# Block products for the upper halves from slice 6 on, and a 64-bit conversion that works in place

## The chip, the cores and the metric

One core of a Trainium2 chip runs the kernel in one launch. The time is the device time of an execution in microseconds. Before the change it is 1780.66 us, the median of three runs (1780.54 to 1782.24).

## The reference

An attention whose softmax runs over the feature axis for q and over the sequence for k makes 2304 tokens of 512 features. A mixture of 8 experts follows, all of them applied to all tokens, weighted by a matrix that eight alternating normalizations make. Last comes a gated feed-forward. All inputs are drawn as below and then cast; `w_in` and `w_out` are 64-bit floats, since they are divided by a 64-bit root.

```python
kv = np.einsum('bhsd,bhse->bhde', k_s, v)
x = np.einsum('bhsd,bhde->bhse', q_s, kv)            # 2304 x 512
for e in range(8):                                   # w1[e] 512 x 1024, w2[e] 1024 x 512
    out += P[:, e:e + 1] * (np.maximum(x @ w1[e], 0.0) @ w2[e])
h = out @ w_in                                       # 512 x 2048, then w_out 2048 x 512
y = (h * np.clip(h + 3.0, 0.0, 6.0) / 6.0) @ w_out
```

## The kernel before

Both feed-forward parts are cut into 20 slices of 512 hidden columns: 16 of the experts (`NE`), 4 of the last layer. For each slice the 18 groups of 128 tokens are taken as three pairs of two groups of 384 tokens. Here a *step* is one pair in one slice; step 14.1 is the second pair taken in slice 14, counted from 0. All operands are float32 numbers split into two float16 halves, an upper and a lower one, so a product is upper x upper plus the two cross products.

The product with W1 (`ups`, L1689) always uses seven block products of half size in place of eight (Strassen-Winograd), in two bursts of seven units a step, 6 matmuls of 384 columns a unit. Each burst leaves four results in float32 rooms (`ring_r`, or parts of `scr`): ACT reads two banks and DVE adds the others. They are split into halves in *ring h*, 16 rooms of two halves, 384 columns each: an upper half by ACT, a lower one by POOL or DVE.

The product with W2 (`downs_fast`, L1867) belongs to the step before and stands between the units of the present one. It uses the seven block products for the cross terms in all of `FAST`. The upper x upper terms are multiplied directly (`main`, L1899), except in the slices of `FULL`, 11 to 14 (L508). There the sums of blocks are made in float32 and split (`whole`, L1766; for W2 `t_sums`, L1458, from sums that POOL leaves in `raw`), and `cross` takes three matmuls a term where it else takes two, without `main`:

```python
def main(o, grp, cols):
    if whole_sums(s, p):
        return
    for fc in range(4):
        nc.tensor.matmul(
            o, hs[grp][fc][:, 0, ts_], w[:, 0, fc, cols], start=False, stop=(fc == 3), skip_group_check=True
        )
```

Whole sums need more rooms, and take six of them in `scr` (L1759). In a FULL slice `raw` holds the float32 sums of W2 up to the end of the slice's first step, so the next weights are prepared one step later in the slice (`when`, L2197).

The 64-bit weights of the last layer are turned to 32 bits on the way, in 32 pieces of 128 x 512 (`conv_steps`, L827): a load into `scr`, four DVE operations, two of ACT, one multiplication on POOL and a store to DRAM (`win`, `wout`). All pieces use the same room. They hang in the queue `back`, from which `tick` (L614) takes one entry on two beats of three; a step has 28 beats. They must be over before slice 16 loads its weights from the result.

Nothing is issued at once: a planner (`Planner`, L73) records every operation with the matmul clock at which it was recorded, finds what depends on what, and lists them by due time with a cost for each form. Background operations (`filling`) are put in only where the due ones behind them still fit (L372), or when their own due time is near. All instructions therefore carry line 471, and the engines run them in the planned order.

Of the kernel before, what the change touches and what calls it, by code (L numbers as in the profile page):

```python
# [474 lines left out]
def tile_attention_moe_ffn(  # L475
# [17 lines left out]
    P = 128  # L493
# [13 lines left out]
    ALSO = ((15, 0), (16, 2))  # L507
    FULL = range(11, 15)  # L508
    PAIRS = [(0, 1), (3, 4), (2, 5)]
# [46 lines left out]
    def psm(shape, name, dt=F32):  # L556
        return bank_of("m", shape)

    def rt(name):
        return ring("r", [P, GN], F32, 6)  # L560
# [245 lines left out]
    def w2_steps(s, flat=raw):  # L806
        st = {}
        dst = w2op[s % 2]
        rw = view(flat, 0, [P, NKC, FS])

        def load():
            nc.sync.dma_start(out=rw, in_=w2_src(s))

        def sp(c):
            return lambda: split(dst[:, 0, c], dst[:, 1, c], rw[:, c], st["s"][:, 0:1])

        steps = [load] + fill(s) + w_scale(f"b{s}_", st, w2buf[s % 2], flat)
        steps[-1] = (lambda f=steps[-1]: (f(), res[s].__setitem__("s2", st["s"])))
        steps += [sp(c) for c in range(NFC)]
        if s in FULL:  # L820
            b11, b12, b21, b22 = w2_parts
            steps += [lambda a=a: nc.gpsimd.tensor_sub(*a) for a in ((b11, b12, b11), (b12, b22, b12), (b22, b11, b22))]
            steps += [lambda: nc.gpsimd.tensor_add(b21, b21, b22)]
        return steps


    def conv_steps(src, dst, name):  # L827

        n = 512
        bits = view(scr, 0, [P, 2 * n], I32).rearrange("p (n t) -> p n t", t=2)  # L830
        hi = bits[:, :, 1]
        mid = view(scr, 0, [P, 2 * n], I32).bitcast(U16).rearrange("p (n t) -> p n t", t=4)[:, :, 1]
        m, t, g = (scr[:, (2 + i) * n : (3 + i) * n] for i in range(3))
        mi, ti = m.bitcast(I32), t.bitcast(I32)

        def load():
            nc.sync.dma_start(out=view(scr, 0, [P, n], U64), in_=src)

        def f0():
# [3 lines left out]
        def f1():  # L843
            nc.scalar.activation(ti, ti, AF.Relu, scale=8.0, bias=less)
            nc.vector.tensor_scalar(
                out=mi, in0=hi, scalar1=0xFFFFF, scalar2=0x100000, op0=ALU.bitwise_and, op1=ALU.bitwise_or
            )

        def f2():
# [4 lines left out]
        def f3():  # L854
            nc.vector.scalar_tensor_tensor(out=m, in0=mi, scalar=2.0 ** -20, in1=g, op0=ALU.mult, op1=ALU.add)

        def f4():
            nc.gpsimd.tensor_mul(m, m, t)

        def store():  # L860
            nc.sync.dma_start(out=dst, in_=m)

        return [load, None, None, f0, f1, f2, f3, f4, None, store]

    def all_conv():
        for i in range(NF):
            fs = slice(i * FS, (i + 1) * FS)
            for c in range(NKC):
                rs = slice(c * P, (c + 1) * P)
                put(back, map(filling, conv_steps(w_in[rs, fs], win32[rs, fs], f"i{i}{c}")))  # L870
            for c in range(NFC):
                rs = slice(i * FS + c * P, i * FS + (c + 1) * P)
                put(back, map(filling, conv_steps(w_out[rs, :], wout32[rs, :], f"o{i}{c}")))
        put(back, [], "conv")
# [38 lines left out]
    def attention(pr):  # L913
# [192 lines left out]
        def qtr(c, g, src=None):  # L1106
# [5 lines left out]
            if "rooms" in t:  # L1112
                qT = t["rooms"][2 + t["m"] % (len(t["rooms"]) - 2)]
            else:
                h = ring("h", [P, 2, GN], F16, HB)
                qT = h.rearrange("p a n -> p (a n)").bitcast(F32)
# [370 lines left out]
    def up_burst(s, p, qf, hs, between):  # L1487
# [36 lines left out]
        def emit(c, grp, fc, clean=False, pool=False):  # L1524
            h = ring("h", [P, 2, GN], F16, HB)
            hs[grp][fc] = h
# [162 lines left out]
    def ups(s, p, hs):  # L1689
# [23 lines left out]
        def gate_(c, grp, fc, scale, bias, top):  # L1713
            h = ring("h", [P, 2, GN], F16, HB)
# [5 lines left out]
        def gated(hg, r, c, pool=True):  # L1720
            h, g, top = hg
            nc.vector.scalar_tensor_tensor(out=r, in0=g, scalar=top, in1=c, op0=ALU.min, op1=ALU.mult)
            nc.scalar.copy(h[:, 0, :], r)
            (nc.gpsimd if pool else nc.vector).tensor_sub(h[:, 1, :], r, h[:, 0, :])

        def straight(b, grp, fc, n, t):

            hg = gate_(b, grp, fc, zd, low3, 6.0 * KAPPA * H_DOWN)
            gated(hg, t(n), b)

# [3 lines left out]
        def hi(c, grp, fc, relu):  # L1734
            h = ring("h", [P, 2, GN], F16, HB)
            hs[grp][fc] = h
# [17 lines left out]
        def burst(qf):  # L1754
            r = [rt(f"r{n}_{s}_{p}_{qf}") for n in range(0)]
            t = {}
# [9 lines left out]
            def whole(which):  # L1766

                for k in which:
# [5 lines left out]
                    elif k == 4:  # L1774
                        r = t[2]
                        if ffn:
                            nc.vector.tensor_add(r, r, t[3])
                        else:
                            nc.vector.scalar_tensor_tensor(
                                out=r, in0=r, scalar=0.0, in1=t[3], op0=ALU.max, op1=ALU.add  # L1780
                            )
                    else:
# [49 lines left out]
            def u5():  # L1832
# [10 lines left out]
            def u6():  # L1843
# [23 lines left out]
    def downs_fast(prev):  # L1867
# [497 lines left out]
```

## Time and profile before

| | before |
|---|---|
| median of 3 runs | 1780.66 us |
| profiled execution | 1781.37 us |
| its span, first to last instruction | 1779.6 us |
| TensorE busy | 1759.3 us (99%) |
| VectorE (DVE) busy | 1377.2 us (77%) |
| ScalarE (ACT) busy | 1193.9 us (67%) |
| GpSimd (POOL) busy | 543.4 us (31%) |

PE is the matmul part of TensorE, PEld its weight loads, SP the engine that issues DMAs. Busy time is the union of an engine's instructions: where two overlap it counts once. An average over the span says little, because the slices differ; so the windows below are cut where the first W1 product of a slice or step starts, and the rest of the reading is by window. A row of windows has the window's bounds and length, then busy time and instructions of PE, PEld, DVE, ACT and POOL, then the granted clock, the DMA share and GB/s. A row of a chain has start, length and what it was; a row of a group has busy time and the mean of one in ns, then the idle time ahead and what ended it.

### The profile page before, as it was taken

How to read it: one execution, taken by the hardware profiler on the slowest of the kernel's cores; microseconds unless marked ns; L12 is line 12 of the kernel's file. 1: busy time of each engine (PE TensorE's matmuls, PEld its weight loads, DVE VectorE, ACT ScalarE, POOL GpSimd, SP SyncE). 2: the span in 40 equal slices, each digit the busy share in tenths (PEclk: the TensorE clock that was granted, in tenths of full speed). 3: DMA queues.
4: the chain of work that ended last, by engine and by line, in shares of the span. 5: the costliest groups of instructions: out<-in, count | busy, mean ns of one | idle time of the engine just before them, and what ended most of it. 6: DMA issues, size and time to landing. Idle time of an engine off the chain costs nothing.

```text
span 1779.6 us, 33317 instructions
## 1 busy us (share of the span) xinstructions
PE 1759.3 (99%) x13097; PEld 1208.3 (68%) x13097; DVE 1377.2 (77%) x2550; ACT 1193.9 (67%) x2654; POOL 543.4 (31%) x513
## 2 busy tenths in 40 slices
PE   7999999999999999999999999999999999999999
PEld 5555556777777777777777777777777555777775
DVE  7874776787777778777866688888888898888774
ACT  5856475666766666766756576867787568876553
POOL 3423344324323232333222222222322223231221
PEclk9999999999999999999999999999999999999999
DMA  9410231324141423142312121120212454302031
GB/s 296 115 68 1 87 99 48 108 80 138 61 134 66 134 66 122 60 140 78 116 62 78 28 84 51 60 81 30 87 48 87 87 95 139 149 25 86 1 98 72
DMA packets 103325, 154.20 MB, mean 87 GB/s; under 512 B 47744, under 2 KB 51840, under 8 KB 102912
## 3 DMA queue, kind: packets, MB, share of 16 engines
q1 hardware_dynamic: 103168, 152.08, 27.7%
q8 instruction: 102, 1.67, 0.4%
q14 instruction: 55, 0.45, 0.1%
HBM read 119.69 MB, written 24.12 MB: 81 GB/s over the span
## 4 chain that ended last, share of the span: by engine, by line
PE 96%; DVE 2%; DMA 1%; ACT 0%; issue 0%; SPq 0%; POOL 0%; ACTq 0%; POOLq 0%
PE b L471 96%; DMA acc<-in_v_dram 0%; DMA raw<-in_moe_w_dram 0%; DVE xbuf L471 0%; DMA xbuf<-in_k_dram 0%; DMA acc<-in_q_dram 0%; DVE ring_r L471 0%; PE b L2331 0%; DVE prob L471 0%; DVE ring_c L471 0%; DVE ring_h L471 0%; DVE ring_qm L471 0%; DVE scr L471 0%; SPq L471 0%; DVE acc L471 0%
## 5 line engine op out<-in xcount | busy, mean ns | idle before, releaser
L471 PE MATMUL b<-xbuf,w1buf 128*128 128x384 f16 x5040 | 908.2, 326 | 1.9 <-ACT ring_r L471 1.2
L471 PEld LDWEIGHTS <-w1buf 128*128 128x128 f16 x5040 | 492.0, 98 | 280.2 <-issue 2.5
L471 PE MATMUL b<-w2buf,ring_h 128*128 128x256 f16 (+1 forms) x3456 | 608.5, 310 | 0.1
L471 POOL TENSOR_TENSOR ring_h<-ring_r,ring_h 128x384 f16<-128x384 f32 x312 | 299.5, 962 | 876.5 <-ACT ring_h L471 727.3
L471 PEld LDWEIGHTS <-ring_h 128*128 128x128 f16 x4116 | 401.2, 98 | 171.6 <-issue 2.1
L471 ACT COPY b<-b 128x256 f32<-128x256 f32 (+1 forms) x686 | 251.6, 375 | 257.3 <-PE b L471 162.1
L471 DVE SCALAR_TENSOR_TENSOR acc<-b,ring_cf,acc 128x512 f32<-128x512 f32 x372 | 274.8, 748 | 143.1 <-PE b L471 126.8
L471 PEld LDWEIGHTS <-xbuf 128*128 128x128 f16 x2820 | 262.9, 98 | 77.3
L471 ACT ACTIVATE ring_r<-b 128x384 f32<-128x384 f32 x384 | 187.5, 489 | 141.7 <-PE b L471 135.4
L471 DVE SCALAR_TENSOR_TENSOR ring_r<-b,ring_r 128x384 f32<-128x384 f32 x250 | 138.0, 553 | 76.4 <-ACT ring_r L471 42.1
L471 ACT ACTIVATE ring_h<-ring_r 128x384 f16<-128x384 f32 x288 | 147.9, 522 | 12.1 <-DVE ring_r L471 8.4
L471 PE MATMUL b<-xbuf 128*128 128x256 f16 (+1 forms) x1236 | 107.3, 249 | 4.1 <-issue 1.7
L471 PE MATMUL b<-kvs,xbuf 128*128 128x256 f16 x660 | 96.1, 273 | 0.0
L471 PE MATMUL b<-scr,xbuf 128*128 128x256 f16 x660 | 96.1, 273 | 0.0
L471 PE MATMUL b<-w2buf,xbuf 128*128 128x256 f16 x660 | 96.1, 273 | 0.0
L471 DVE TENSOR_TENSOR xbuf<-ring_h 128x768 f16<-128x768 f16 x148 | 91.4, 620 | 0.0
L471 DVE SCALAR_TENSOR_TENSOR acc<-b,ring_co,acc 128x512 f32<-128x512 f32 (+1 forms) x82 | 60.5, 742 | 30.7 <-PE b L471 27.6
L471 ACT CAST ring_h<-ring_r 128x384 f16<-128x384 f32 x144 | 72.0, 508 | 17.4 <-DVE ring_r L471 16.5
L471 PE MATMUL b<-xbuf,ring_h 128*128 128x256 f16 x366 | 80.0, 273 | 0.0
L471 DVE SCALAR_TENSOR_TENSOR w1buf<-raw,ring_ws,w1buf 128x512 f16<-128x512 f32 x100 | 76.3, 794 | 2.1 <-ACT w1buf L471 1.5
L471 PE MATMUL b<-lg,ring_h 128*128 128x256 f16 x294 | 74.1, 273 | 0.0
L471 ACT ACTIVATE w1buf<-raw,ring_ws 128x512 f16<-128x512 f32 x100 | 67.9, 715 | 6.6 <-DVE ring_ws L471 5.8
(185 smaller groups left out, 1802.9 us busy)
## 6 DMA issues: line engine op xcount, KB each, us to landing
xbuf<-xkeep SPq DMA_DIRECT2D x119, 384.0 KB, 3.7
raw<-in_moe_w_dram SPq DMA_DIRECT2D x31, 1024.0 KB, 5.8
scr<-in_moe_w_in_dram SPq DMA_DIRECT2D x16, 512.0 KB, 3.6
scr<-in_moe_w_out_dram SPq DMA_DIRECT2D x16, 512.0 KB, 3.4
xkeep<-xbuf SPq DMA_DIRECT2D x2, 2688.0 KB, 8.9
xkeep<-xbuf SPq DMA_DIRECT2D x14, 384.0 KB, 7.7
out_dram<-acc SPq DMA_DIRECT2D x18, 256.0 KB, 2.0
win<-scr SPq DMA_DIRECT2D x16, 256.0 KB, 2.1
```

The lines of the kernel that those rows point to most:

```text
L471: f(*a, **k)
```

## The change

`FULL` becomes slices 6 to 14. Three things follow from code that depends on it: whole sums and no `main` in slices 6 to 10, later preparation of weights for slices 6 to 11, and no room in `scr` for the conversion from slice 6 on.

- *Halves that nothing multiplies are not made.* With whole sums, block 21 of the hidden values enters sums alone, so its halves are dropped; block 12 is clipped in place by ACT, its upper half made by ACT and the lower by POOL (before: ACT, then DVE). Of W2, one quarter, block 12, enters sums alone, and the split of its rows covers half the width.
- *The conversion in place.* A piece takes 3 x 512 words where it took 5 x 512: the masks and sums go back into the strided words of the loaded numbers. Until slice 6 a piece stands in `scr`. From the third step of slice 6 it stands in the last four rooms of ring h, which `ht` keeps from the halves while `lending` is 2 or 3; with 6 halves a step instead of 8, twelve rooms hold two steps. `lend` moves the state on before each step, at slice 15 all pieces still open are recorded, and the rooms go back to ring h. While pieces are lent rooms, one entry is taken on one beat of four.

```diff
-    FULL = range(11, 15)
+    FULL = range(6, 15)
+    def ht(s):
+        if "h" not in rings:
+            rings["h"] = [cpool.tile([P, HB, 2, GN], F16, name="ring_h"), list(range(HB))]
+        r, last = rings["h"]
+        n = next(n for n in last if n < HB - 4 or lending[0] in (0, 1, 4))
+        last.append(last.pop(last.index(n)))
+        return r[:, n]
...
-        if back and beat[0] % 3:
+        if back and (chunk[0] or lending[0] in (0, 3)) and (
+            beat[0] % 4 < 1 if lending[0] else beat[0] % 3 < 2
+        ):
             pop(back)
...
+        if s in FULL and s < NS - 1:
+            left = slice(0, DM // 2)
+            steps += [sp(0), sp(1)]
+            steps += [lambda: split(dst[:, 0, 2:, left], dst[:, 1, 2:, left], rw[:, 2:, left], st["s"][:, 0:1])]
...
+                    st["at"] = scr if not lending[0] else rings["h"][0][:, HB - 4 :].rearrange(
+                        "p b a n -> p (b a n)"
+                    ).bitcast(F32)
...
-            nc.vector.scalar_tensor_tensor(out=m, in0=mi, scalar=2.0 ** -20, in1=g, op0=ALU.mult, op1=ALU.add)
+            nc.vector.scalar_tensor_tensor(out=g, in0=hi, scalar=2.0 ** -20, in1=g, op0=ALU.mult, op1=ALU.add)
...
-            nc.gpsimd.tensor_mul(m, m, t)
+            nc.gpsimd.tensor_mul(t, g, t)
...
-                    after_units(1, lambda: lo(hi(t[4], 0, qf + 2, False), t[4], False))
+                    if not full:
+                        after_units(1, lambda: lo(hi(t[4], 0, qf + 2, False), t[4], False))
...
-                    if full:
-                        lo(hi(t[2], 1, qf, True), t[2], True)
-                        return
                     nc.scalar.activation(t[2], t[2], AF.Relu)
                     lo(hi(t[2], 1, qf, False), t[2], False)
...
+    def lend(s, p):
+        n = turns[s].index(p)
+        at = 0 if s < FULL[0] else 4 if s >= 15 else min(n + 1, 3) if s == FULL[0] else 3
+        while back and at != lending[0] and (at == 4 or chunk[0]):
+            pop(back)
+        lending[0] = at
```

On PE, in slice 8, the product for the lower token group of one tile stood before as two cross matmuls a term and then the wide ones (`lg` and `xbuf` hold the two parts of T4, `w2buf` is W2, bank b_67 the sum):

```order
L471 MATMUL b_67<-lg,ring_h 128x256
L471 LDWEIGHTS ring_h
L471 MATMUL b_67<-xbuf,ring_h 128x256
L471 LDWEIGHTS ring_h
L471 MATMUL b_67<-w2buf_83,ring_h 128x512
L471 LDWEIGHTS ring_h
L471 MATMUL b_67<-w2buf_83,ring_h 128x512
```

The same place now:

```order
L472 MATMUL b_67<-lg,ring_h 128x256
L472 LDWEIGHTS ring_h
L472 MATMUL b_67<-xbuf,ring_h 128x256
L472 LDWEIGHTS ring_h
L472 MATMUL b_67<-xbuf,ring_h 128x256
L472 LDWEIGHTS ring_h
L472 MATMUL b_67<-lg,ring_h 128x256
```

The four wide matmuls are gone, and each of the two terms has a third narrow one.

On DVE, at the start of slice 15 (`acc` is the result of the W2 products, `xbuf` the halves of sums, `ring_r` and `scr` results of the W1 products, `ring_h` of 384 columns a lower half), before:

```order
L471 SCALAR_TENSOR_TENSOR acc<-b_67,ring_cf,acc 128x512
L471 SCALAR_TENSOR_TENSOR acc<-b_66,ring_cf,acc 128x512
L471 TENSOR_TENSOR ring_wsc<-ring_ws 128x1
L471 TENSOR_SCALAR ring_cf<-prob,ring_wsc 128x18
L471 TENSOR_TENSOR xbuf<-ring_r,xbuf 128x384
L471 TENSOR_TENSOR xbuf<-scr,xbuf 128x384
L471 TENSOR_TENSOR xbuf<-ring_r,xbuf 128x384
L471 SCALAR_TENSOR_TENSOR ring_h<-ring_r,ring_h 128x384
L471 SCALAR_TENSOR_TENSOR ring_h<-scr,ring_h 128x384
L471 SCALAR_TENSOR_TENSOR ring_r<-ring_r 128x384
```

Now, where `ring_h` of 512 columns is a piece of the conversion in its lent rooms:

```order
L472 SCALAR_TENSOR_TENSOR acc<-b_67,ring_cf,acc 128x512
L472 SCALAR_TENSOR_TENSOR acc<-b_66,ring_cf,acc 128x512
L472 TENSOR_SCALAR ring_ws<-ring_c1i 128x1
L472 TENSOR_TENSOR ring_wsc<-ring_ws 128x1
L472 TENSOR_SCALAR ring_cf<-prob,ring_wsc 128x18
L472 SCALAR_TENSOR_TENSOR ring_h<-ring_h 128x512
L472 TENSOR_TENSOR xbuf<-scr,xbuf 128x384
L472 TENSOR_TENSOR xbuf<-ring_r,xbuf 128x384
L472 TENSOR_SCALAR ring_h<-ring_h 128x512
L472 SCALAR_TENSOR_TENSOR ring_h<-ring_h 128x512
L472 TENSOR_TENSOR xbuf<-scr,xbuf 128x384
L472 TENSOR_TENSOR xbuf<-ring_r,xbuf 128x384
```

Three of the four operations of a piece have come in between the sums, and the two lower halves stand elsewhere or are gone.

## Rows read from the trace of the kernel before

**Rows 1.** Page, shares of the span and granted clock by slice of it

```profile
PE 1759.3 (99%) x13097; PEld 1208.3 (68%) x13097; DVE 1377.2 (77%) x2550; ACT 1193.9 (67%) x2654; POOL 543.4 (31%) x513
...
PEclk9999999999999999999999999999999999999999
```

**Rows 2.** Page, chain that ended last; then the largest group of matmuls

```profile
PE 96%; DVE 2%; DMA 1%; ACT 0%; issue 0%; SPq 0%; POOL 0%; ACTq 0%; POOLq 0%
...
L471 PE MATMUL b<-xbuf,w1buf 128*128 128x384 f16 x5040 | 908.2, 326 | 1.9 <-ACT ring_r L471 1.2
```

**Rows 3.** Windows: slices 4, 12, 13, 16, and 2 to 9 together

```profile
412.88:497.08 84.20, 84.20 (x617) 59.97 (x615) 64.76 (x118) 57.09 (x131) 27.56 (x27) 1.00 0.32 102
1083.99:1166.56 82.57, 82.49 (x634) 61.73 (x632) 69.92 (x127) 61.68 (x147) 22.83 (x20) 1.00 0.20 60
1166.56:1248.89 82.33, 82.33 (x634) 61.74 (x632) 69.66 (x128) 61.41 (x147) 23.14 (x20) 1.00 0.20 60
...
1418.67:1507.68 89.01, 88.32 (x476) 46.22 (x474) 81.75 (x161) 63.47 (x115) 26.89 (x24) 1.00 0.53 120
...
242.71:918.07 675.36, 675.36 (x4869) 475.51 (x4868) 514.14 (x924) 455.90 (x1044) 233.13 (x226) 1.00 0.30 97
```

**Rows 4.** Start of slice 15: PE's wait; first and last of the chain's DVE pieces

```profile
1342.69 1.14 PE L471 MATMUL b<-xbuf,w1buf 128*128 128x384 f16 x6 [1.19 <-ACT ring_r L471]
...
1331.42 0.19 DVE ring_r L471
...
1339.99 2.13 DVE xbuf L471 x3
```

**Rows 5.** Groups of PE by form in slice 4 (busy us, mean ns)

```profile
L471 PE MATMUL b<-w2buf,ring_h 128*128 128x512 f16 x36 | 9.2, 379 | 0.0
```

**Rows 6.** A group of DVE by form in slices 11 to 14: lower halves

```profile
L471 DVE SCALAR_TENSOR_TENSOR ring_h<-ring_r,ring_h 128x384 f16<-128x384 f32 x23 | 12.7, 568 | 0.0
```

**Rows 7.** Chain of waits in slice 12 (start, us, what)

```profile
1138.22 6.57 DMA raw<-in_moe_w_dram
```

**Rows 8.** Groups by form: conversion on DVE and POOL, dearest 512-column DVE row

```profile
L471 DVE TENSOR_SCALAR scr<-scr 128x512 int32<-128x512 int32 x60 | 29.3, 498 | 0.0
L471 DVE SCALAR_TENSOR_TENSOR scr<-scr 128x512 int32<-128x512 int32 x30 | 22.3, 745 | 4.5 <-ACT scr L471 4.5
L471 DVE SCALAR_TENSOR_TENSOR scr<-scr 128x512 f32<-128x512 int32 x31 | 21.3, 688 | 0.7
...
L471 POOL TENSOR_TENSOR scr<-scr 128x512 f32<-128x512 f32 x32 | 42.0, 1312 | 46.5 <-DVE scr L471 42.5 <-ACT ring_r L471 4.0
...
L471 DVE SCALAR_TENSOR_TENSOR scr<-raw,ring_ws,scr 128x512 f16<-128x512 f32 x4 | 3.7, 929 | 0.0
```

**Rows 9.** Windows: steps 13.2, 14.0, 14.1, 14.2, 15.0, 15.1 and 16.1

```profile
1221.44:1248.89 27.45, 27.45 (x212) 20.59 (x211) 25.03 (x49) 21.14 (x54) 4.74 (x5) 1.00 0.14 39
1248.89:1276.29 27.40, 27.40 (x212) 20.55 (x210) 22.55 (x37) 17.88 (x42) 8.75 (x8) 1.00 0.27 76
1276.29:1303.76 27.47, 27.47 (x213) 20.60 (x211) 22.08 (x43) 22.39 (x54) 9.65 (x8) 1.00 0.21 66
1303.76:1331.22 27.46, 27.46 (x213) 20.60 (x211) 24.81 (x48) 22.46 (x55) 4.14 (x5) 1.00 0.22 68
1331.22:1360.03 28.81, 27.62 (x214) 20.61 (x211) 25.92 (x47) 21.70 (x52) 10.80 (x9) 1.00 0.27 83
1360.03:1389.43 29.40, 29.40 (x219) 21.20 (x218) 22.09 (x40) 19.77 (x48) 6.61 (x8) 1.00 0.16 59
1447.92:1478.06 30.14, 29.45 (x159) 15.39 (x158) 29.04 (x64) 23.05 (x39) 7.63 (x7) 1.00 0.58 97
```

**Rows 10.** SP: first converted weights for slice 16; page: conversion DMAs

```profile
1327.38 0.37 SPq L471 DMA_DIRECT2D raw<-win  x1
...
scr<-in_moe_w_in_dram SPq DMA_DIRECT2D x16, 512.0 KB, 3.6
...
win<-scr SPq DMA_DIRECT2D x16, 256.0 KB, 2.1
```

More of the change, by code (lines that the diff above doesn't have):

```diff
@@ L59 @@
     "a1sums": -73500.0,
+    "conv": 0000.0,
     "max": 40000.0,
@@ L607, in tile_attention_moe_ffn @@
     rate = [1]
+    chunk = [False]
+    lending = [0]
     def pop(d):
@@ L818, in w2_steps @@
         steps[-1] = (lambda f=steps[-1]: (f(), res[s].__setitem__("s2", st["s"])))
-        steps += [sp(c) for c in range(NFC)]
+        if s in FULL and s < NS - 1:
+            left = slice(0, DM // 2)
+            steps += [sp(0), sp(1)]
+            steps += [lambda: split(dst[:, 0, 2:, left], dst[:, 1, 2:, left], rw[:, 2:, left], st["s"][:, 0:1])]
+        else:
+            steps += [sp(c) for c in range(NFC)]
         if s in FULL:
@@ L829, in conv_steps, with room, g, load @@
         n = 512
[L830 to L839, printed above, removed]
+        st = {}
+        def room(f):
+            def g():
+                if f is load:
+                    st["at"] = scr if not lending[0] else rings["h"][0][:, HB - 4 :].rearrange(
+                        "p b a n -> p (b a n)"
+                    ).bitcast(F32)
+                    chunk[0] = True
+                lent = st["at"]
+                bits = lent[:, : 2 * n].bitcast(I32).rearrange("p (n t) -> p n t", t=2)
+                hi = bits[:, :, 1]
+                mid = lent[:, : 2 * n].bitcast(U16).rearrange("p (n t) -> p n t", t=4)[:, :, 1]
+                g, t = bits[:, :, 0].bitcast(F32), lent[:, 2 * n : 3 * n]
+                marked(filling(lambda: f(lent, hi, mid, g, t, t.bitcast(I32))), "conv")()
+                if f is store:
+                    chunk[0] = False
+            return g
+        def load(lent, *_):
+            nc.sync.dma_start(out=lent[:, : 2 * n].bitcast(U64), in_=src)
+        def f0(lent, hi, mid, g, t, ti):
             nc.vector.tensor_scalar(out=ti, in0=hi, scalar1=0x7FF00000, scalar2=None, op0=ALU.bitwise_and)
             nc.scalar.activation(g, mid, AF.Copy, scale=2.0 ** -36)
-        def f1():
+        def f1(lent, hi, mid, g, t, ti):
             nc.scalar.activation(ti, ti, AF.Relu, scale=8.0, bias=less)
[L845 to L849, printed above, removed]
+        def f2(lent, hi, mid, g, t, ti):
             nc.vector.scalar_tensor_tensor(
@@ L852, in f2, with f3, f4, store @@
             )
-        def f3():
-            nc.vector.scalar_tensor_tensor(out=m, in0=mi, scalar=2.0 ** -20, in1=g, op0=ALU.mult, op1=ALU.add)
-        def f4():
-            nc.gpsimd.tensor_mul(m, m, t)
-        def store():
-            nc.sync.dma_start(out=dst, in_=m)
-        return [load, None, None, f0, f1, f2, f3, f4, None, store]
+            nc.vector.tensor_scalar(
+                out=hi, in0=hi, scalar1=0xFFFFF, scalar2=0x100000, op0=ALU.bitwise_and, op1=ALU.bitwise_or
+            )
+        def f3(lent, hi, mid, g, t, ti):
+            nc.vector.scalar_tensor_tensor(out=g, in0=hi, scalar=2.0 ** -20, in1=g, op0=ALU.mult, op1=ALU.add)
+        def f4(lent, hi, mid, g, t, ti):
+            nc.gpsimd.tensor_mul(t, g, t)
+        def store(lent, hi, mid, g, t, ti):
+            nc.sync.dma_start(out=dst, in_=t)
+        return [f and room(f) for f in (load, None, None, f0, f1, f2, f3, f4, None, store)]
     def all_conv():
@@ L869, in all_conv @@
                 rs = slice(c * P, (c + 1) * P)
-                put(back, map(filling, conv_steps(w_in[rs, fs], win32[rs, fs], f"i{i}{c}")))
+                put(back, conv_steps(w_in[rs, fs], win32[rs, fs], f"i{i}{c}"))
             for c in range(NFC):
                 rs = slice(i * FS + c * P, i * FS + (c + 1) * P)
-                put(back, map(filling, conv_steps(w_out[rs, :], wout32[rs, :], f"o{i}{c}")))
+                put(back, conv_steps(w_out[rs, :], wout32[rs, :], f"o{i}{c}"))
         put(back, [], "conv")
@@ L1114, in qtr @@
             else:
-                h = ring("h", [P, 2, GN], F16, HB)
+                h = ht(0)
                 qT = h.rearrange("p a n -> p (a n)").bitcast(F32)
@@ L1524, in emit @@
         def emit(c, grp, fc, clean=False, pool=False):
-            h = ring("h", [P, 2, GN], F16, HB)
+            h = ht(s)
             hs[grp][fc] = h
@@ L1713, in gate_ @@
         def gate_(c, grp, fc, scale, bias, top):
-            h = ring("h", [P, 2, GN], F16, HB)
+            h = ht(s)
             hs[grp][fc] = h
@@ L1718, in gate_, with gated @@
             return h, g, top
-        def gated(hg, r, c, pool=True):
+        def gated(hg, r, c, pool=True, split_=True):
             h, g, top = hg
             nc.vector.scalar_tensor_tensor(out=r, in0=g, scalar=top, in1=c, op0=ALU.min, op1=ALU.mult)
+            if not split_:
+                return
             nc.scalar.copy(h[:, 0, :], r)
@@ L1728, in straight @@
             hg = gate_(b, grp, fc, zd, low3, 6.0 * KAPPA * H_DOWN)
-            gated(hg, t(n), b)
+            gated(hg, t(n), b, split_=not full or n == 1)
         def around(r, grp, fc, pool=True):
@@ L1734, in hi @@
         def hi(c, grp, fc, relu):
-            h = ring("h", [P, 2, GN], F16, HB)
+            h = ht(s)
             hs[grp][fc] = h
@@ L1754, in burst @@
         def burst(qf):
-            r = [rt(f"r{n}_{s}_{p}_{qf}") for n in range(0)]
             t = {}
@@ L1775, in whole @@
                         r = t[2]
[L1776 to L1781, printed above, removed]
+                        nc.vector.tensor_add(r, r, t[3])
                     else:
@@ L1973, in downs_fast @@
         return made
+    def lend(s, p):
[4 more added lines that the diff above has]
+        lending[0] = at
     def fast_step(s, p, prev):
+        lend(s, p)
         need(("w1", s))
```

## The prediction

> **What bounds the kernel now.** I read the page's shares first, then the chain of waits, then busy time in windows cut at the first product of each 512-column slice, and last the DVE groups by form. TensorE is busy for 99% of the span and its granted clock is full from end to end, so its 2.4 GHz level holds throughout [rows 1]. The chain that ended last runs through PE for 96%, and the largest group of matmuls waited 1.9 us in the whole run [rows 2]. So PE's own columns set the time, and a helper engine matters only where it makes PE stand. The windows say how near that is. In slice 4, where the upper halves are multiplied directly, the window is 84.20 us and PE has no gap. In slice 13, as in 14, where seven block products are already used for them, it is 82.33 us, again without a gap, and DVE is busy for 85% of it (69.66 us) [rows 3]. At slice 15 PE does wait: 1.19 us for a room that ACT fills, behind ten microseconds, from 1331.4 to 1342.1 us, in which the chain has 11 pieces of DVE and no other engine [rows 4].
>
> **The columns that go.** One tile of 128 tokens in a direct slice has 7 cross products of 4 x 256 columns and the main ones of 4 x 512 and 8 x 256: 11,264 columns. With whole sums it has 7 x 6 x 256 = 10,752. The 512 columns saved are 213 ns at 2.4 GHz, and a slice has 9 tiles: 1.92 us. The 36 wide matmuls of a slice that vanish are the 512-column row of slice 4 [rows 5]. The windows give nearly the same by measurement: 84.20 - 82.33 = 1.87 us. Slices 6 to 10 change, 5 x 1.87 = 9.35 us. All of it is on PE, so all of it counts where PE doesn't wait.
>
> **What rides along in slices 6 to 12.** The work there becomes that of slices 12 to 14 without their two dead halves. In each burst the half of block 21 is not made (one ACT write, one POOL subtraction), and that of block 12 goes from one ACT and one DVE instruction to two ACT and one POOL: ACT and POOL come out even, DVE loses one row of 0.57 us per burst [rows 6], 2.3 us in four bursts. Half a W2 split per slice goes as well. DVE at 85% with no gap in slices 13 and 14 is the cover; I cost these slices at nothing. Earlier preparation of the weights moves to the second and third step of a slice, as in slices 11 to 14. There the load of one W2 slice once stood in the chain for 6.57 us and cost PE 0.08 us of slice 12 (82.49 of 82.57), because ACT had that slice's sums queued ahead of a bank copy [rows 3, 7]. Five more such slices could each show that: 0 to 2 us, and I take 0.5.
>
> **Where the conversion goes.** By the order of the changed program, 20 of the 32 pieces stay in the old room and are done in slices 2 to 5, some 6 a slice where there were some 4.4 (32 in slices 2 to 9). Slice 4 had DVE at 64.76 of 84.20 us [rows 3]; 1.6 pieces more, at 2.43 us each (below), make 68.7 us, 82%: no cost. Of the other 12, the planner puts nearly nothing into slices 6 to 12 (one instruction here and there), because a background operation only enters where the due ones behind it still fit. Then their room is due: the four rooms of ring h are wanted again in slice 15, and pieces that share one room stand one behind the other. So the order has 37 of their 48 DVE instructions in the five steps from 13.2 to 15.0 (step n.m is the m-th pair of slice n, from 0): 5, 8, 8, 8, 8. The excerpts of DVE's order shown above are one such place, and it is the very stretch of [rows 4], where DVE already sets PE's time.
>
> The sum there: one piece costs DVE two masks of 0.498, one of 0.745 and one of 0.688 us, 2.43 us, and POOL 1.31 us [rows 8]. No row shows them in the strided, in-place form. The bounds are 2.0 us (all four at the masks' 0.498) and 3.7 us (four times the dearest row of 512 elements, 0.929 us [rows 8]), which would put 9 us over full DVE into three steps, the size of rival 2. The inputs were strided before, so I take 2.43. Steps 14.1, 14.2 and 15.0 last 83.7 us and DVE is busy in them for 22.08 + 24.81 + 25.92 = 72.8 us [rows 9]. Less 2.3 us of dead halves, plus six pieces, 14.6 us, makes 85.1 us: 102% of the time there is. Steps 13.2 and 14.0: 47.6 - 2.3 + 7.9 = 53.2 of 54.9 us, 97%. The highest share a step shows is 16.1 with 29.04 of 30.14 us, 96% [rows 9], and slice 16 as a whole has 81.75 of 89.01 us, 92% [rows 3], both with 0.69 us in which PE stood. At 96.3%, 85.1 us take 88.4 us and 53.2 us take 55.2: 4.6 + 0.4 = 5.0 us over PE's time. At 91.8% they take 92.7 and 58.0 us: 9.0 + 3.1 = 12.1 us. The lower end is nothing, if DVE's lag runs out in step 15.1, which has 7 us to spare (22.09 of 29.40) and PE's rooms carry it there. Step by step the stall is one of the order in which DVE stands, so it is nearest to the row of the one crowded step, 96%; some of it can be carried over, and I take 4.5 us. ACT in 15.0 is busy for 21.70 of 28.81 us [rows 9] and gets four rows more: no bound by itself.
>
> Behind a late DVE instruction stand the additions that read a bank of PE; PE's next product into that bank is what waits. The queue of SP carries the pieces' loads and stores in front of two things: the first converted weights for slice 16, issued at 1327.38 us where their first product starts at 1418.67 [rows 10, 3], so some 85 us of cover, and the reload of the third pair in slice 15, a step of cover.
>
> **The sum.** Profiled execution: 1781.37 us (span 1779.6). -9.35 + 0.5 + 4.5 = -4.35 us, 1777.0. The median of the three runs is 0.7 us under the profiled one, so 1776.3 us.
>
> **Rivals.** (1) *The crowd costs nothing.* The planner gives each background row a place that its model thinks free, and before, all 32 pieces went through slices 2 to 9, 675.36 us in which PE had no gap [rows 3]. Against it is 102% in three steps. 1780.66 - 9.35 = 1771.3. (2) *DVE becomes the bound at 92%.* 1780.66 - 9.35 + 0.5 + 12.1 = 1783.9. For it: 1.19 us at 15.0 with DVE at only 90%. Against: only 9 pieces are crowded, and in 16.1 DVE reached 96%. (3) *The rooms come back late*, slower than before: slice 15 writes its first halves into just the four lent rooms, and ACT stands at that write, with the bank copies behind it, until POOL's last product is over and, for two of the rooms, its store has landed. The pieces go at two a step, so one that misses its turn is 27.5 / 2 = 13.7 us late; 1780.66 - 9.35 + 13.7 = 1785.0. It decides from the point where ACT reaches the first of these writes before the twelfth piece's product has ended. Against: a piece needs about 3.6 us of load, 2.4 of DVE, 1.3 of POOL and 2.1 of store [rows 8, 10], some 9.4 of its 13.7 us. (4) *Matmuls count, not columns.* The change puts 6 matmuls for every 4, 90 more in all. At 84.20 us / 617 rows = 136 ns each that would be 12.3 us more: 1793. The rows speak against it: slice 13 has 634 rows in 82.33 us, slice 4 has 617 in 84.20.
>
> The Trainium skill, in "TensorE: Matmul & The Clock Gate", section "Back-to-back issue gap", gives for streams of weight load and matmul a sustained spacing of about 81 ns at 128 columns and 131 ns at 512. An estimate for 256 columns between these is 98 ns, so six of them for four wide ones would cost 588 for 524 ns, 2.9 us more over 45 tiles, some 1783.6 us in all. The trace disagrees, by the windows just named; the other figure of that section of the Trainium skill, columns / 2.4 plus 2.5 ns, would give the 1.87 us that the windows show.
>
> **How the numbers follow.** A difference under 0.2%, 3.6 us, counts as none (what a measurement of this kernel can tell): faster is below 1777.1, slower above 1784.2. The forecast, 1774 to 1779, has 0.50; rival 1 (1770.5 to 1774) 0.25; rival 2 (1779 to 1784) 0.13; rival 3 0.10; rival 4 0.02. Two thirds of the forecast's chance lies below 1777.1: 0.33 + 0.25 = 0.58 faster. The rest of it and rival 2: 0.30 the same. Slower: 0.12. The range goes from the full saving with a little more from the lighter steps, 1770.5, to most of rival 2, 1783.
>
> **What would show it.** Windows of slices 7 to 12 should last 82.3 to 82.7 us without gaps, with DVE at 82 to 85%; if they last 84, rival 4 holds. Steps 13.2 to 15.0 should together be 3 to 6 us longer than 138.6 us, with PE's waits released by DVE or by ACT behind DVE, and DVE at 95% or more. If those steps are as long as before, the crowd was free and the forecast is too high. If one wait of over 5 us stands in 15.0 with ACT waiting to write ring h, rival 3 holds. If slices 3 to 5 get longer, the denser conversion was not free, which I have at nothing.

## The result, and the profile after

| | before | after |
|---|---|---|
| median | 1780.6 us (6 runs) | 1793.41 us (6 runs, 1792.55 to 1798.79) |
| ratio | | 1.007, 95% interval 1.0057 to 1.0083 |
| profiled execution, its span | 1781.37, 1779.6 us | 1792.56, 1790.8 us |

The change made the kernel slower by 0.7%, where 0.2% faster was forecast, and the time lies above the range of 1770.5 to 1783 us. The page of the changed kernel, against [rows 1, 2]:

```profile
PE 1756.8 (98%) x13187; PEld 1216.8 (68%) x13187; DVE 1429.6 (80%) x2632; ACT 1233.4 (69%) x2755; POOL 556.4 (31%) x503
...
PE 93%; DVE 3%; DMA 1%; ACT 1%; issue 0%; POOL 0%; SPq 0%; POOLq 0%
...
L472 PE MATMUL b<-xbuf,w1buf 128*128 128x384 f16 x5040 | 912.5, 327 | 5.2 <-DVE ring_r L472 2.6
```

PE is busy for 2.5 us less, and yet the span is 11.2 us longer: PE stands, that is, it waits for another engine. DVE is busy for 52 us more. The windows of slices 5, 8, 12, and 13 to 16, with columns as in [rows 3]:

```profile
497.00:582.13 85.13, 84.46 (x615) 59.92 (x614) 71.16 (x124) 57.76 (x135) 35.12 (x33) 1.00 0.38 116
...
747.21:829.54 82.33, 82.33 (x635) 61.72 (x633) 69.73 (x123) 60.58 (x144) 23.82 (x20) 1.00 0.20 60
1077.55:1159.88 82.33, 82.33 (x635) 61.72 (x633) 67.01 (x123) 62.80 (x147) 22.67 (x20) 1.00 0.21 60
1159.88:1243.51 83.63, 83.63 (x645) 62.88 (x644) 70.01 (x126) 62.21 (x146) 23.24 (x20) 1.00 0.23 70
1243.51:1330.26 86.75, 80.93 (x611) 59.03 (x609) 75.98 (x140) 65.61 (x152) 31.86 (x26) 1.00 0.39 115
1330.26:1426.77 96.51, 91.14 (x600) 59.02 (x598) 81.72 (x145) 61.39 (x133) 26.53 (x24) 0.96 0.41 104
1426.77:1518.88 92.11, 88.99 (x475) 46.09 (x474) 81.92 (x163) 63.57 (x115) 25.42 (x24) 1.00 0.50 115
```

Slice 8 has exactly the 82.33 us of the whole-sum slices. Slices 6 to 12 together went from 585.3 to 577.8 us (-7.5). Slices 3 to 5 went from 252.6 to 254.1 (+1.5). Slices 13 to 16 went from 341.1 to 359.0: +17.9 us, all of the loss and more; 14.2 of it are in steps 13.2 to 15.0, which took 152.8 us for the same 1056 matmuls where they took 138.6. The steps 14.1, 14.2 and 15.0, against [rows 9]:

```profile
1269.61:1300.32 30.71, 27.93 (x212) 20.57 (x211) 26.53 (x52) 23.28 (x55) 10.78 (x9) 1.00 0.36 110
1300.32:1330.26 29.94, 26.89 (x202) 19.11 (x200) 28.00 (x52) 23.98 (x56) 9.22 (x9) 1.00 0.36 102
1330.26:1368.81 38.55, 33.65 (x237) 23.73 (x235) 33.20 (x58) 27.16 (x63) 15.66 (x13) 0.91 0.41 127
```

DVE is busy for 26.53 + 28.00 + 33.20 = 87.7 us of 99.2: 88%, not 96%. By step it is 86, 94 and 86%. Inside 15.0, in windows of a few us:

```profile
1330.00:1340.00 10.00, 9.90 (x77) 7.27 (x76) 9.93 (x19) 8.75 (x22) 3.44 (x3) 1.00 0.46 155
1340.00:1345.00 5.00, 1.96 (x16) 1.03 (x13) 4.96 (x8) 2.12 (x8) 3.53 (x3) 1.00 0.13 24
1345.00:1350.00 5.00, 3.23 (x12) 1.64 (x13) 4.75 (x11) 1.76 (x4) 1.09 (x1) 0.57 0.39 134
1350.00:1352.00 2.00, 2.00 (x11) 1.36 (x10) 0.59 (x1) 1.87 (x4) 0.00 (x0) 0.50 0.00 0
```

DVE is full for 20 us (19.64 busy) while PE gets 5.2 of the ten from 1340, and right behind that DVE has next to nothing to do (0.59 of 2 us): its next additions need banks that PE could not fill. In the table of DVE's waits for 15.0 (us, times, longest) that is the largest entry:

```profile
DVE acc L472 <- PE b L472: 4.1, 4, 1.6
```

So the two engines stand in turn, and much of the 12% of DVE that the windows show as free is time in which DVE itself waits. PE's rows at the spot (start, us, tiles, idle before):

```profile
1341.91 0.50 PE L472 MATMUL b<-xbuf 128*128 128x256 f16 x3 [1.01 <-DVE xbuf L472]
...
1346.56 1.25 PE L472 MATMUL b<-scr,xbuf 128*128 128x256 f16 x5 [2.52 <-DVE xbuf L472]
1348.01 2.08 PE L472 MATMUL b<-xbuf,w1buf 128*128 128x384 f16 x6 [0.21 <-ACT ring_r L472]
```

The last row takes 2.08 us where the same six products take 1.14 [rows 4]: the granted clock, full up to here, is at its lower level (1.2 GHz) for 6.8 us after these waits (0.57 and 0.50 in the windows). PE worked in 5.8 of them, and half of that, 2.9 us, is what the clock cost. What DVE did meanwhile, and what POOL did, in two lists:

```profile
1341.30 0.55 DVE L472 TENSOR_TENSOR xbuf<-scr,xbuf 128x384 f16<-128x384 f32 x1
1341.77 1.65 DVE L472 TENSOR_TENSOR xbuf<-ring_r,xbuf 128x384 f16<-128x384 f32 x1
...
1343.41 1.55 DVE L472 TENSOR_TENSOR ring_r<-ring_r 128x384 f32<-128x384 f32 x1
1344.88 1.62 DVE L472 TENSOR_TENSOR xbuf<-scr,xbuf 128x384 f16<-128x384 f32 x1
```

```profile
1341.47 1.54 POOL L472 TENSOR_TENSOR ring_h<-ring_h 128x512 f32<-128x512 f32 x1 [3.05 <-DVE ring_h L472]
1342.97 1.57 POOL L472 TENSOR_TENSOR wtmp<-wtmp,raw 128x512 f32<-128x512 f32 x1
1344.51 1.58 POOL L472 TENSOR_TENSOR raw<-raw 128x512 f32<-128x512 f32 x1
```

A sum on DVE takes 0.55 us; the three that start while a POOL operation on two inputs runs take 1.55 to 1.65 us, and end 0.4 us behind it. `ring_h<-ring_h` is the product of a lent piece, `wtmp` and `raw` are the sums of slice 16's W1. The Trainium skill, "SBUF — State Buffer", section "Who interferes with whom", says that a DVE instruction with two SBUF inputs contends with a GpSimd instruction that reads SBUF, that contention for the port pair they share is an exclusive lock, and that issue order decides who blocks. These rows agree: the DVE row of 1341.30, which started before POOL's, took its 0.55 us.

PE's gaps in slices 13 to 16 come to 14.3 us (5.8, 5.4 and 3.1 in 14, 15 and 16) where they were 1.9. With 2.9 us of clock that is 12.4 + 2.9 = 15.3 of the 17.9. Most of the other 2.6 us may be what restarts cost: PE stands 14 times there where it stood twice, and a single product of 256 columns fills 0.27 us where the next follows after 0.11, so each restart adds some 0.16 us that counts as busy, 1.9 us in all (an estimate from those rows).

### The profile page after: what moved, and what is told of

The parts are those of the page before. It is cut to its first block, busy times and chain, and to the rows that moved or that the text cites. A ratio compares the mean times of both kernels' runs of the same rounds, so it can differ in the third digit from the quotient of the medians.

```text
span 1790.8 us, 33679 instructions
## 1 busy us (share of the span) xinstructions
PE 1756.8 (98%) x13187; PEld 1216.8 (68%) x13187; DVE 1429.6 (80%) x2632; ACT 1233.4 (69%) x2755; POOL 556.4 (31%) x503
## 4 chain that ended last, share of the span: by engine, by line
PE 93%; DVE 3%; DMA 1%; ACT 1%; issue 0%; POOL 0%; SPq 0%; POOLq 0%
PE b L472 93%; DVE xbuf L472 1%; DVE scr L472 1%; DVE ring_r L472 0%; DMA acc<-in_v_dram 0%; DMA raw<-in_moe_w_dram 0%; DVE acc L472 0%; DMA acc<-in_q_dram 0%; ACT xbuf L472 0%; PE b L2368 0%; DVE ring_h L472 0%; DMA xbuf<-in_k_dram 0%; DVE w2buf L472 0%; ACT w2buf L472 0%; DVE prob L472 0%
## 5 line engine op out<-in xcount | busy, mean ns | idle before, releaser
L472 PE MATMUL b<-w2buf,ring_h 128*128 128x256 f16 (+2 forms) x3096 | 532.6, 309 | 0.3 <-ACT b L472 0.2
L472 POOL TENSOR_TENSOR ring_h<-ring_r,ring_h 128x384 f16<-128x384 f32 x270 | 271.1, 1006 | 750.1 <-ACT ring_h L472 656.2
L472 PEld LDWEIGHTS <-ring_h 128*128 128x128 f16 x3846 | 374.8, 98 | 160.7 <-issue 3.8
L472 PEld LDWEIGHTS <-xbuf 128*128 128x128 f16 x3180 | 298.2, 98 | 85.3 <-DVE xbuf L472 7.4
L472 ACT ACTIVATE ring_r<-b 128x384 f32<-128x384 f32 x324 | 157.4, 488 | 116.9 <-PE b L472 110.2
L472 DVE SCALAR_TENSOR_TENSOR ring_r<-b,ring_r 128x384 f32<-128x384 f32 x220 | 121.6, 553 | 68.1 <-PE b L472 33.9
L472 ACT ACTIVATE ring_h<-ring_r 128x384 f16<-128x384 f32 x210 | 107.6, 522 | 6.7 <-DVE ring_r L472 4.3
L472 POOL TENSOR_TENSOR raw<-raw 128x512 f32<-128x512 f32 x56 | 76.6, 1369 | 65.6 <-DVE w2buf L472 26.9
L472 POOL TENSOR_TENSOR ring_h<-scr,ring_h 128x384 f16<-128x384 f32 x36 | 36.6, 1018 | 178.3 <-ACT ring_h L472 178.3
L472 DVE TENSOR_TENSOR xbuf<-scr,xbuf 128x384 f16<-128x384 f32 x116 | 71.0, 633 | 8.0 <-ACT xbuf L472 7.8
```

The costliest lines, as they stand in the source:

```text
L472: f(*a, **k)
```

## The experiments

Theories: **A**, the forecast's, that DVE carries pieces for nothing up to some 96% and the loss lies elsewhere (rooms back late, DMAs); **B**, that each piece crowded into 13.2 to 15.0 costs PE time through DVE; **C**, that POOL's operations beside DVE's rows do it. Later a fourth: **D**, that step 15.0 itself is the dear place.

Two things hold for all of them. In the 20 profiled executions the stretch ahead of the first W1 product took from 44.5 to 50.5 us, by no pattern of the edits, while slices 17 and 18 took 82.30 and 86.32 us in every one: what an edit does is read from the slices, and the time of a single run says little within 5 us. And each edit makes the planner write a new order for every engine, so a run compares two orders; none takes rows out of an order that is otherwise kept.

**1. The lent pieces without their arithmetic**, loads and stores kept:

```diff
+        def unless_lent(f):
+            return lambda *a: f(*a) if st["at"] is scr else None
+        work = [unless_lent(f) for f in (f0, f1, f2, f3, f4)]
...
```

> The changed kernel, in which the 12 pieces in lent rooms are only loaded and stored, without their DVE, ACT and POOL operations (so 12 of 32 pieces of the last layer's weights are not converted). Crowd (48 DVE rows of the pieces, 37 of them in steps 13.2 to 15.0, make PE stand, and the fall of the clock in slice 15 follows from that): 1771 to 1774 us, slice 14 at 82.3 us, slice 15 at 87.5, granted clock full. Rooms (ACT stands because the lent rooms come back late): the loads and stores still pass through the rooms, so some of slice 15's 9 us stays, 1776 to 1782. Nine slices of whole sums are too much in themselves: 1790 or more.

1782.06 us, ratio 0.9996 (0.9985 to 1.0007). Slices 13 to 16 are back at 343.1 us, with the clock full: the loss comes with the pieces' arithmetic, not with their loads and stores, which stay. But slices 8 to 14 had a wait of 0.57 us each:

```profile
746.42:829.48 83.06, 82.49 (x635) 61.76 (x632) 68.53 (x122) 60.77 (x144) 22.91 (x20) 1.00 0.25 79
...
1327.83:1415.76 87.93, 86.27 (x587) 57.08 (x586) 74.12 (x130) 56.51 (x123) 22.29 (x21) 1.00 0.36 87
```

**2. The same without POOL's share of the lent pieces alone** (`f4` left out of them):

```diff
...
+        return [f and room(f) for f in (load, None, None, f0, f1, f2, f3, unless_lent(f4), None, store)]
```

> The changed kernel, in which the 12 lent pieces are not multiplied by POOL (their last step is left out, so they are wrong), with all DVE and ACT rows kept: 33 of 48 DVE rows of the pieces stand in 14.0 to 15.0. Crowd by DVE's own rows alone: slices 13 to 16 stay near 359 us, at least 355. If POOL's 1.46 us of two-input product a piece, which keeps DVE's two-input rows waiting, is a good part of it: 345 to 354 us. Without pieces these slices took 343.1, before the change 341.1.

1787.75 us (one run), slices 13 to 16 355.3: 3.7 us less than in the changed kernel. But 2.8 of these are in slice 16, which holds no piece, and slices 13 to 15 together gained 0.95 us. So where the pieces stand, POOL's product is worth about 1 us of the 16, and the rest stays.

**3. The 0.57 us.** Two runs on top of experiment 1, the first with the W2 split at full width again, the second with block 12's halves made by ACT and DVE again:

```diff
-        if s in FULL and s < NS - 1:
+        if False:
```

> As the run whose lent pieces are only loaded and stored (12 of 32 pieces not converted), and the split of W2 covers the full width again, as before the change. That run had one stall of 0.57 us a slice in slices 8 to 14, at the slice's third microsecond, where DVE's two-input rows took 1.62 us instead of 0.55 beside 3.2 us of POOL's W2 sums. If the lighter split brought the sums to that place: the stall goes, slices 8 to 14 are 82.33 us. If block 12's way over ACT and POOL did: it stays, 83.06 us.

```diff
...
+                    if full:
+                        lo(hi(t[2], 1, qf, True), t[2], True)
+                        return
```

> As the run whose lent pieces are only loaded and stored (12 of 32 pieces not converted), and block 12's halves go their old way: the upper one by ACT from the unclipped sum, the lower one by DVE. If block 12's way over ACT and POOL put POOL's W2 sums beside DVE's rows at the start of a slice: slices 8 to 14 go from 83.06 to 82.33 us. If the lighter W2 split did: they stay at 83.06.

1774.2 and 1773.42 us (one run each), slices 8 to 14 at 82.33 us in both. Either edit alone takes the wait away, so neither of the two lighter forms makes it by itself. In experiment 1 a POOL sum of W2 stands beside a DVE sum there that takes 1.62 us; in these two no DVE sum at that place is lengthened. That this is an accident of the planner's order is argued. These two show what the whole sums are worth with twelve pieces left undone.

**4. Every piece early**, one queue entry on every beat, 29 pieces in slices 2 to 5:

```diff
-            beat[0] % 4 < 1 if lending[0] else beat[0] % 3 < 2
+            True
```

> The changed kernel, with one entry of the conversion taken on every beat (two of three before) until slice 6: 29 pieces fall into slices 2 to 5, and 3 into lent rooms, one DVE row at a time up to step 13.0; no DVE row of a piece stands in 13.1 to 15.0. Crowd: slices 14 and 15 as before the change, so 1771 to 1775 us; what slices 2 to 5 lose is some 9 more pieces of 2.4 us over 340 us in which DVE was busy for 80%: 0 to 4 us. Nine slices too much in themselves: 1790.

1792.45 us, 1.0062 (1.0045 to 1.0079). The loss moved: slices 14 to 16 are within 0.5 us of before, slice 3 lasts 92.55 us with DVE at 80.47, also 87%.

```profile
332.48:425.03 92.55, 88.03 (x632) 61.12 (x631) 80.47 (x141) 64.96 (x150) 37.68 (x33) 1.00 0.43 128
```

**5. Whole sums from another slice.** From 11 as before, with all the rest of the change; then from 8:

```diff
-    FULL = range(6, 15)
+    FULL = range(11, 15)
```

> The changed kernel with whole sums from slice 11 on, as before the change: what is left of the change is the halves that are not made and the conversion in place, all 32 pieces of it in the old room, before slice 11. If the strided rows of the pieces or their denser order cost anything, it shows here alone: more than 1782 us. Crowd: 1779 to 1781, same as before the change, since PE's columns are the same and the lighter DVE hides.

> The changed kernel with whole sums from slice 8 on: 30 of 32 pieces are converted in slices 2 to 7, in the old room, and the rest one DVE row at a time up to 12.0. Three slices get whole sums instead of five. Crowd: no crowd is left, so 1780.7 less 3 x 1.87 plus what the seven slices of the new order lose to a stall of 0.57 each, 0 to 4: 1775 to 1780 us. If a piece costs about 1 us of PE wherever it stands: 1781 to 1786.

1786.81 us, 1.0027 (1.0016 to 1.0039), without one more whole-sum slice: the new code costs by itself, in waits of 0.4 to 0.6 us in slices 10, 11, 13 and 14, and of 1.7 us in 15.0, where it was 1.2. One of them, DVE and then PE:

```profile
1167.19 1.62 DVE L472 SCALAR_TENSOR_TENSOR ring_h<-ring_r,ring_h 128x384 f16<-128x384 f32 x1
1168.74 1.62 DVE L472 TENSOR_TENSOR ring_r<-ring_r 128x384 f32<-128x384 f32 x1
...
1171.47 0.81 PE L472 MATMUL b<-xbuf,w1buf 128*128 128x384 f16 x4 [0.57 <-DVE ring_r L472]
```

POOL runs two W2 sums there, 3.20 us from 1166.74. From 8: 1783.15 us, 1.0008 (0.9998 to 1.0017); PE's gaps in the denser slices 5, 6 and 8 are 2.6, 1.1 and 1.3 us, where there were none.

**6. One piece a step.** The lent pieces due 13.5 us apart, so that 12.0 to 15.0 have one a step:

```diff
+    **{f"conv{j}": (11 - j) * 13500.0 for j in range(12)},
...
```

> The changed kernel, with the due times of the 12 late pieces set 13.5 us apart more than they were, the first the earliest: 4 DVE rows in each step from 12.0 to 15.0 where there were 5, 8, 8, 8, 8 in 13.2 to 15.0. Same work in all. Crowd: DVE needs some 22.5 + 2.4 us of 27.4 in each step, 91%, which PE has borne elsewhere; most of the 12 us over the sum come back, 1773 to 1780. If it is the sum of DVE work and not where it stands that costs: 1788 to 1793.

1786.02 us, 1.003 (1.0021 to 1.004). Slices 12 to 14 lost 5 us in sum, slice 15, with one piece in 15.0, 4.2 us.

**7. Half the pieces.** Every second lent piece without arithmetic:

```diff
+                    st["idle"] = bool(lending[0]) and lent_so_far[0] % 2 == 0
...
```

> Every second of the twelve pieces in lent rooms does none of its DVE, ACT and POOL work, so six pieces are left unconverted; loads and stores stay. In steps 14.0 to 15.0 the order then has 13 DVE rows of pieces instead of 32, one piece a step from 14.1. Measure: slices 13 to 16 together (341.1 us before, 359.0 changed, 343.1 with no piece converted). If every crowded piece costs PE about the same (16 us / 12 = 1.3 us), 350 to 352 us. If there is a point below which DVE carries pieces for nothing (my forecast's sum: DVE at up to 96%), one piece a step is below it: 343 to 344 us. If the loads and stores in the lent rooms were the cost, 359 us.

1780.0 us, slices 13 to 16 345.5: +4.4 us, not half of 17.9. Six pieces cost a quarter of what twelve do, and all but 0.5 us of it in slice 15. Steps 14.1, 14.2 and 15.0, one piece in each:

```profile
1270.70:1298.16 27.46, 27.46 (x213) 20.60 (x211) 21.80 (x39) 22.80 (x54) 10.77 (x9) 1.00 0.38 126
1298.16:1325.62 27.46, 27.46 (x213) 20.61 (x211) 24.16 (x49) 21.32 (x52) 7.10 (x5) 1.00 0.31 98
1325.62:1356.37 30.75, 28.63 (x214) 20.15 (x212) 26.71 (x48) 23.26 (x56) 13.42 (x9) 1.00 0.46 152
```

The same piece is free in 14.1 and 14.2; with it 15.0 is 1.9 us longer than before [rows 9], at 87% of DVE, and 15.1 has 1.5 us of gaps behind it. B in the form "so much a piece" falls, and theory D stands for these steps; by experiment 6 other steps are not always free at one piece.

**8. What makes 15.0 dear.** POOL's four sums of slice 16's W1 left out, from the changed kernel and from that of experiment 7:

```diff
-            return lambda: getattr(nc.gpsimd, fn)(o, a, b)
+            return lambda: None if s == NE else getattr(nc.gpsimd, fn)(o, a, b)
```

> The changed kernel without POOL's four sums of slice 16's W1 blocks, which step 15.0 prepares; all twelve pieces and their work stay. In 15.0 five DVE rows took over 1 us, 4.6 us more than at 0.55 us each. If those collisions make the step dear, PE's gaps in slice 15 fall from 5.4 us to 1 or 2, the clock stays full there, and the slice lasts 88 to 90 us instead of 96.5; slice 14 keeps its 5.8 us. If it is DVE's amount of work, slice 15 stays at 94 to 97 us.

> The kernel in which every second lent piece does no arithmetic, and again without POOL's four sums of slice 16's W1 blocks. There one piece stood in 15.0 and slice 15 lasted 91.4 us with 3.65 us of gaps. If POOL's sums beside DVE's rows were their cause, slice 15 lasts 87 to 88.5 us; if the one piece was, it stays at 90 to 92 us.

Half the pieces (1773.58 us, one run): slice 15 fell from 91.41 us with 3.65 of gaps to 86.39 without any. All pieces (1798.64 us, one run, with 5 us more ahead of slice 0 and 3.7 us more in slice 16): slice 15 fell from 96.5 to 93.2, its gaps from 5.4 to 3.2 us, and slice 14 kept gaps of 6.3 us where the changed kernel has 5.8. Slice 15 in both, and step 15.0 of the first:

```profile
1323.74:1410.13 86.39, 86.36 (x587) 57.09 (x585) 72.95 (x139) 58.56 (x129) 20.18 (x19) 1.00 0.42 108
1323.74:1351.39 27.65, 27.62 (x213) 20.59 (x211) 25.03 (x51) 22.80 (x56) 6.94 (x5) 1.00 0.54 174
```

```profile
1335.92:1429.10 93.18, 90.00 (x600) 58.58 (x598) 78.03 (x143) 59.52 (x131) 20.19 (x20) 0.98 0.36 94
```

So at one piece in 15.0 the price is POOL's sums beside DVE's rows (C), and DVE is busy there for 91% of the step (25.03 of 27.65 us) without a gap. At two a step waits are left. POOL's products of the pieces still run in these steps, so C is not out of them; but the longest wait in 14.1 of the changed kernel has another face:

```profile
1278.41 2.11 PE L472 MATMUL b<-xbuf,w1buf 128*128 128x384 f16 x12 [1.80 <-ACT ring_r L472]
...
1270.37 0.66 DVE xbuf L472
1271.03 0.66 DVE scr L472
1271.69 0.66 DVE kvs L472
1272.35 0.67 DVE lg L472
```

From 1269.8 us up to this wait DVE has no row of a piece, and POOL runs one row of 1.08 us. The four DVE rows are sums of W2's blocks; before, four other rows stood among them (1274.06 to 1279.70), now they stand in a block in front of the sums that PE needs. So the crowd also acts by what it pushes aside in the planned order; that the eight piece rows of 14.0 pushed these four is argued. B in the plain form, DVE's amount of work, is not separated from this by any run, and the two ACT operations of a piece were never left out alone.

**9. All pieces, spread, none in 15.0**: due 13.5, 27 and 20 us apart, and 40 to 45 us sooner; the fourth is the second with block 12 as before:

```diff
+    **{f"conv{j}": (11 - j) * 27000.0 + 40000.0 for j in range(12)},
...
```

> The twelve lent pieces are due 13.5 us apart and 40 us sooner: one piece a step from 11.2 to 14.2, none in 15.0. If the place (15.0) is what is dear, slices 11 to 14 last 82.3 to 82.7 us and slice 15 87.9: 1780.7 - 9.4 + 1.5 (slices 3 to 5) + 1 = 1774 us. If a piece costs as where one stood in every step before (5 us in slices 12 to 14), 1778 to 1779 us. If every crowded or uncrowded piece costs 1.3 us, 1788 us.

> The same with the pieces due 27 us apart: at most two pieces a slice from 9.1 to 14.2, none in 15.0. By the place or by the density 1773 to 1775 us, below the kernel before. If a piece costs 1 us in a whole-sum slice wherever it stands, 1783 to 1785 us.

> The same with the pieces due 20 us apart and 45 us sooner: from 10.1 to 14.1, so that 14.2 is free too. By the place 1773 to 1775 us; by density between the two runs beside it; by 1 us a piece 1783 us.

> The pieces 27 us apart as in the second run, and block 12's halves made by ACT and DVE as before. That edit alone took a stall of 0.57 us out of every whole-sum slice when no lent piece was converted. If DVE's total is what counts, this one is slower than the second run by 1 us or more (a DVE row of 0.57 us a burst); if the order of POOL's sums is, equal or faster: 1772 to 1774 us.

Beside 1781.28 us of before, in this order: 1780.4 (ratio 0.9987 to 1.0007), 1779.7 (0.998 to 0.9999), 1783.74 (0.9992 to 1.0015) and 1789.49 us (1.002 to 1.0059). The same twelve pieces, with all their arithmetic, cost 17.7 us over slices 12 to 16 in the changed kernel and 4.7 us in the first of these:

```profile
1077.17:1163.68 86.51, 84.78 (x653) 63.49 (x651) 75.33 (x138) 66.49 (x156) 33.95 (x25) 1.00 0.26 85
...
1328.84:1416.58 87.74, 86.99 (x594) 57.62 (x592) 73.25 (x135) 57.47 (x126) 21.59 (x21) 1.00 0.38 97
```

The second is the only version whose interval lies below the kernel before, by 0.1%, within what the prediction counts as none. Slices 2 to 18, without the ends that vary, took 1433.6 us before, 1445.5 in the changed kernel and 1432.6 and 1432.7 in the first two. Most of the forecast 9.35 us is spent there on some 6 us in slices 10 to 15 and 1.5 in 3 to 5. The fourth refutes experiment 3 as a remedy: the edit that took waits away there gave slices 10 and 12 gaps of 3.7 and 4.2 us here.

**10. Whole sums from 8 and 9 with the old block 12**, the middle one with the old W2 split too; nearly all pieces stand in `scr`:

> Whole sums in slices 8 to 14, block 12's halves made by ACT and DVE as before, the conversion in place as changed. All pieces but one or two stand in scr in slices 2 to 7. If the short stalls of whole-sum slices come only from where the order puts POOL's sums against DVE, slices 8 to 14 last 82.33 us as they did with all pieces' arithmetic gone, so three slices save 5.6 us and the conversion costs 1 to 2 us in slices 3 to 7: 1776 to 1777 us. If a denser conversion always costs what it lets the whole sums save, 1781 to 1784 us as without this edit (1783.2).

> The same with the split of W2 at its full width too, as before. Both undone, whole-sum slices 8 to 14 are those of the kernel before, three slices earlier: 1776 to 1777 us if the stalls are the order's, 1781 to 1784 us if the conversion eats the saving. DVE has about 1 us more a slice than in the run beside it, so if DVE's load itself were the cost, this one would be the slower of the two.

> Whole sums in slices 9 to 14, block 12 as before; all 32 pieces stand in scr, 7 of them (28 DVE rows) in slice 8, the last direct one. Two slices save 3.7 us. If six to seven pieces in a direct slice are free or nearly so, 1777 to 1778 us; if they cost about 1 us each beyond five a slice, as in the run with every piece in slices 2 to 5, 1780 to 1783 us.

1782.99 us (ratio 1.0002 to 1.0024), 1790.19 (1.0034 to 1.0068) and 1780.72 (0.9982 to 1.0006). Slices 10 and 12 to 14 last 82.33 us in all three; what is saved is lost in slices 3 to 9, most of which take the pieces: they stand 4.6, 6.3 and 2.4 us over the sum of 84.20 us for a direct slice and 82.33 us for one of whole sums. In the second, seven DVE rows of late pieces in 15.0 cost slices 15 and 16 4.3 and 3.1 us.

## Why the prediction was wrong

**The columns** were right: 82.33 us in slices 7 and 8, with 635 matmuls for 617. Rival 4 is refuted: that its 1793 us is nearly the measured 1793.41 is chance, since the loss is not in these slices. The sustained spacing that the Trainium skill gives in "TensorE: Matmul & The Clock Gate", section "Back-to-back issue gap", and that I had weighed there, does not fit these windows either.

**Slices 6 to 12** stand 1.4 us over seven times 82.33, 0.4 of it in slice 6, which still changes over; I had 0.5. So slices 6 to 10 gave 8.3 us.

**The denser conversion in slices 2 to 5**, which I had at nothing, cost 1.5 us: slice 5 has 71.16 us of DVE and 0.67 of gaps. 80 to 84% of DVE (slices 3 and 5) is not a cover by itself.

**The step that failed is the crowd's price**: "At 96.3%, 85.1 us take 88.4 us". The place was right, and the loss did not come from more work than I had: in steps 13.2 to 15.0 DVE was busy for 131.9 us, where my sum has 85.1 + 53.2 = 138.3, and a piece's four rows took 2.23 us, where I had 2.43. Yet those steps lost 14.2 us, where the sum has 5.0 and takes 4.5. What was wrong is to turn a busy share into a time. 96% was the highest share that any step showed, and I used it as a capacity. DVE's instructions stand in one order with those that need PE's banks and those that PE needs. When it is late, PE stands, and then it waits for PE itself; the crowded steps reached 86 to 94% (slice 3 of experiment 4: 87%; step 15.0 of experiment 7: 87%), while 15.0 of experiment 8 ran at 91% without a wait. No one share would have given the time: it depends on which rows stand in front of those that PE needs, and beside which POOL operations. Rival 2, at 92% and 12.1 us, was the nearest.

**What I had not in the sum.** POOL's operations had a price only on POOL; beside DVE's sums they are DVE's time, some 1.0 us each. The planner has this lock in its model (`lock`, L246 and L370) and plans no such rows side by side; in the runs they met all the same. The trace of before had it at the very place of [rows 4], in DVE's own list, beside a sum of POOL's from 1337.49 of 1.62 us; I read the chain there, in which such a row looks like work:

```profile
1337.90 1.62 DVE L471 SCALAR_TENSOR_TENSOR ring_h<-scr,ring_h 128x384 f16<-128x384 f32 x1
```

The clock fell for 6.8 us after PE's waits, 2.9 us. And slice 16, which got no piece, had 3.1 us of gaps where it had 0.7: the planner wrote DVE's rows there in another order. Experiment 10's second kernel has the same 3.1 us, others 0.7 or 0.8. What brings that order is open: experiment 2, with eight piece rows in 15.0 as well, has 0.8 us there.

**Rival 3** did not happen: ACT's longest wait in 15.0 was 2.8 us, for a sum of DVE's and not for a room.

## What to carry to other kernels

Where two engines feed each other in fixed orders, the busy share that a helper reached in its best stage is not a capacity: late steps here had shares from 86 to 94%, and one at 91% had no wait. Before background work is laid into a step, look at what POOL does there: a two-input operation of its own beside a DVE row took some 1.0 us of DVE's time, and one piece was free in one step and made the next 1.9 us longer. Where a planner writes the order, read the new order too: what the background work pushes aside can land in front of the rows that matter. A saving on the bounding engine is worth what is left after the work that it pushes elsewhere is placed; here 9 us were bought with twelve pieces that cost 5 us well spread and 18 in a crowd.

## What the runs showed of the hardware

- DVE rows with both inputs in SBUF took 1.55 to 1.65 us instead of 0.55 beside POOL's operations of 1.5 to 1.6 us, and as short a row as 128 x 18 took 1.33 us in experiment 7 just before its wait in 15.0.
- After waits of 1.0, 1.1 and 2.5 us within six microseconds PE's clock fell to its 1.2 GHz level for 6.8 us; after waits of 1.0 and 1.7 us in experiment 2 for 3.4 us. Single waits went both ways: after 1.8 and 2.2 us in slice 14 of the changed kernel it did not fall, after 1.84 us in 15.0 of the third run of experiment 9, with no other wait in that step before it, it fell for 3.4 us.
